# One PSUM tile for each row tile of a down product, in a state-space and SwiGLU kernel on one core

## The chip, the cores and the metric

The kernel runs on one core of a Trainium2 chip. The metric is the device time of one launch in microseconds. A kernel is timed in several runs; the profile is of one further execution, which has a time of its own.

## The reference, cut to what matters

Four layers follow each other on a row of 2048 positions with 512 channels: a state-space convolution (A), a SwiGLU feed-forward product (B), and both again with the same weights.

```python
x = A_u                                        # 1 x 2048 x 512
for _ in range(2):
    x = x + A(layernorm(x))                    # y = irfft(rfft(x) * rfft(K)), K from A, B, C, dt; + x * Dskip
    n = layernorm(x)
    x = x + (silu(n @ w_gate) * (n @ w_up)) @ w_down     # 512 -> 1376 -> 512
```

## The kernel before, in words

**Stages.** About the first 320 us make the convolution kernel, transform it, and split the weights into pairs of 16-bit halves. Behind it lie eight pairs of a convolution and a feed-forward product, in the order of the table `SEQ`: a layer and a block of 512 positions each. The loop at the end of the listing calls `ssm` for the next pair (all of it, line by line of the program) and then `ffn` for the present one, so that VectorE works on the convolution of one block while TensorE works on the feed-forward product of the block before.

**The order.** Nothing from there on is in an order written by hand. A scheduler with a timeline of its own sorts the instructions of each engine at build time: by program order, with the instructions under `tc.high_priority` ahead, and with whatever is ready by its own reckoning put into a wait. On the chip each engine then runs its list strictly in that order. So a change of one dependence moves many instructions on every engine.

**The feed-forward product.** `ffn` takes a block in two subtiles of 256 positions (`s`), each of two row tiles of 128 positions (`r`). For one subtile:

- `ffn_norm` normalizes the rows, splits them into two halves `nh` and `nlo`, and has them transposed by DMA (L841, tile `mix<-nn`).
- Gate and up: six groups `f0` of columns, each into a PSUM tile `pgu` of two banks. The group `FT - 1` is the remainder of 96 columns (`remainder`, L853 to L855, 48 matmuls with 96 columns); the other five have 48 matmuls with 256 columns (L886 to L888). Behind each group stands a chain: ScalarE silu (L891), VectorE product (L892), ScalarE cast into `hh` (L893), VectorE difference into `hl` (L894); for the remainder L861 to L864 and four transposing DMAs (L867).
- Down: for each row tile 33 matmuls with 512 columns (L900, L901, L902: eleven blocks `f` by three products of halves) into PSUM. Then VectorE adds the result to the rows `xt` (L905, called the eviction here), and a DMA writes them out (L907 in the last layer, else L909).

**PSUM.** The eight banks are shared by two tags. `sml` has four tiles of one bank, used by the convolution's products `pf` (L270) and `pi` (L781). `big` has two places of two banks each. Every `pgu` takes one of the two places, and so does the tile `py` of a down product: `py` has a bank for each of the two row tiles. A place is free for the next tile when all readers of the last one are done. A matmul into a tile, and a read of it by another engine, are ordered by the framework.

In `ffn` of the listing the groups stand in the order remainder, 0, 2, 4, 6, 8, then the down product. The last groups' chain must end before the down product's blocks 8 and 9 can be multiplied.

Of the kernel before, what the change touches and what calls it, by code (L numbers as in the profile page):

```python
# [16 lines left out]
OP = mybir.AluOpType  # L17
# [4 lines left out]
L, D, F = 2048, 512, 1376  # L22
P = 128
T = 512
NB = L // T
FT = 11
# [55 lines left out]
def kernel(ctx, tc, x, a_re, a_im, b_re, b_im, c_re, c_im, log_dt, d_skip,  # L82
                           w_gate, w_up, w_down, c_ef, c_ei, c_ek, c_am, c_eh, c_eih, out):
    nc = tc.nc
    V, A, G, PE = nc.vector, nc.scalar, nc.gpsimd, nc.tensor
# [9 lines left out]
    def tl(shape, name, tag, dt=F32):  # L95
        return sb.tile(shape, dt, name=name, tag=tag, bufs=BUFS[tag])

    def pbig(shape, name):
        return ps.tile(shape, F32, name=name, tag="big", bufs=2)
# [33 lines left out]
    sc6 = sb.tile([P, 6], F32, name="sc6")  # L133
# [158 lines left out]
    def second(h, q, space=psml):  # L292
        n = []
        for cp in range(2):
            t = tl([P, 2, HD], "n1", "w")
            nc.sync.dma_start(t, ndr[h, cp])
            n += [t[:, 0], t[:, 1]]
        return direct(1, h, q, n, space)
# [327 lines left out]
    def wgu(wi, kc, lo, n=1):  # L626
        u = 8 * wi + 4 * lo + kc
        v = wsl[u // 6].rearrange("p (u f) -> p u f", u=6)
        return v[:, u % 6] if n == 1 else v[:, u % 6:u % 6 + n]

    def wd(fc, lo):
        r = 2 * fc + lo
        if r < 5:
            return wsl[2][:, 4 * F + r * D:4 * F + (r + 1) * D]
        return wsl[3][:, (r - 5) * D:(r - 4) * D] if r < 21 else wx
# [177 lines left out]
    def ffn_norm(layer, b, s, wait=None):  # L813


        rows = TB // P
        xt = xs[SEQ.index((layer, b)) % 3][:, s * rows:(s + 1) * rows]
        nh, nlo = nhl2[:, s % 2, 0], nhl2[:, s % 2, 1]
        with tc.high_priority(offset=BOOST):
            if wait:  # L820
                rs, nb = stats(xt, rows, 256.0, "stats2")
                pt = pbig([P, rows, 4, P], "pt")
                for r in range(rows):
                    nn = nn2[:, r]
                    A.activation(nn, xt[:, r], AF.Identity, scale=rs[:, r:r + 1], bias=nb[:, r:r + 1])
                    for k in range(4):
                        PE.transpose(pt[:, r, k], nn[:, k * P:(k + 1) * P], ident)
                ptv = pt.rearrange("p r k t -> p k r t")
                nhv = nh.rearrange("p k (r t) -> p k r t", r=rows)
                A.activation(nhv, ptv, AF.Copy)  # L830
                wait()
                V.tensor_tensor(nlo.rearrange("p k (r t) -> p k r t", r=rows), ptv, nhv, OP.subtract)  # L832
                return nh, nlo
            rs, nb = row_stats(xt, rows, 256.0, "stats2", lambda r: nn2[:, r])
            nt = nn2[:, 1].bitcast(F16).rearrange("p (i k) -> p i k", i=2)
            for r in range(rows):
                A.activation(nn2[:, 0], xt[:, r], AF.Identity, scale=rs[:, r:r + 1], bias=nb[:, r:r + 1])
                A.activation(nt[:, 0], nn2[:, 0], AF.Copy)
                V.tensor_tensor(nt[:, 1], nn2[:, 0], nt[:, 0], OP.subtract)
                for i, o in enumerate((nh, nlo)):  # L840
                    nc.sync.dma_start_transpose(o[:, :, r * P:(r + 1) * P], nt[:, i])  # L841
        return nh, nlo

    def remainder(pgu, nh, nlo, hh, hl):

        rows = TB // P
        fs = slice(F - FR, F)
        pr = pgu.rearrange("p a b t -> p (a b t)")[:, :rows * 2 * FR].rearrange("p (r w f) -> p r w f", r=rows, w=2)
        for r in range(rows):
            rc = slice(r * P, (r + 1) * P)  # L850
            for wi in range(2):
                for k in range(4):
                    PE.matmul(pr[:, r, wi], lhsT=nh[:, k, rc], rhs=wgu(wi, k, 0)[:, fs], start=k == 0, stop=False)  # L853
                    PE.matmul(pr[:, r, wi], lhsT=nh[:, k, rc], rhs=wgu(wi, k, 1)[:, fs], start=False, stop=False)
                    PE.matmul(pr[:, r, wi], lhsT=nlo[:, k, rc], rhs=wgu(wi, k, 0)[:, fs], start=False, stop=k == 3)  # L855
        with tc.high_priority(offset=BOOST):
            both = tl([P, 2, TB], "sgr", "sg")
            sg = both[:, 0, :rows * FR].rearrange("p (r f) -> p r f", r=rows)
            hs = both[:, 1].bitcast(F16).rearrange("p (l r f) -> p l r f", l=2, r=rows)
            G.memset(hs[:, :, :, FR:], 0.0)  # L860
            A.activation(sg, pr[:, :, 0], AF.Silu, scale=sc6[:, 3:4])  # L861
            V.scalar_tensor_tensor(sg, pr[:, :, 1], sc6[:, 4:5], sg, OP.mult, OP.mult)
            A.activation(hs[:, 0, :, :FR], sg, AF.Copy)
            V.tensor_tensor(hs[:, 1, :, :FR], sg, hs[:, 0, :, :FR], OP.subtract)  # L864
            for i, o in enumerate((hh, hl)):
                for r in range(rows):
                    nc.sync.dma_start_transpose(o[:, FT - 1, r * P:(r + 1) * P], hs[:, i, r])  # L867

    def ffn(layer, b, ready=None):
        for s in range(T // TB):  # L870
            rows = TB // P
            xt = xs[SEQ.index((layer, b)) % 3][:, s * rows:(s + 1) * rows]
            nh, nlo = ready if ready and s == 0 else ffn_norm(layer, b, s)
            hh = tl([P, FT, TB], "hh", "hh", F16)
            hl = tl([P, FT, TB], "hl", "hl", F16)
            for f0 in (0, 2, 4, 6, FT - 1, 8) if ready and s == 0 else (FT - 1, 0, 2, 4, 6, 8):
                pgu = pbig([P, 2, 2, TB], "pgu")
                if f0 == FT - 1:
                    remainder(pgu, nh, nlo, hh, hl)
                    continue  # L880
                for i in range(2):
                    fs = slice((f0 + i) * P, (f0 + i + 1) * P)
                    for wi in range(2):
                        o = pgu[:, wi, i]
                        for k in range(4):
                            PE.matmul(o, lhsT=wgu(wi, k, 0)[:, fs], rhs=nh[:, k], start=k == 0, stop=False)  # L886
                            PE.matmul(o, lhsT=wgu(wi, k, 0)[:, fs], rhs=nlo[:, k], start=False, stop=False)  # L887
                            PE.matmul(o, lhsT=wgu(wi, k, 1)[:, fs], rhs=nh[:, k], start=False, stop=k == 3)  # L888
                with tc.high_priority(offset=BOOST):
                    sg = tl([P, 2, TB], "sg", "sg")  # L890
                    A.activation(sg, pgu[:, 0], AF.Silu, scale=sc6[:, 3:4])  # L891
                    V.scalar_tensor_tensor(sg, pgu[:, 1], sc6[:, 4:5], sg, OP.mult, OP.mult)  # L892
                    A.activation(hh[:, f0:f0 + 2], sg, AF.Copy)  # L893
                    V.tensor_tensor(hl[:, f0:f0 + 2], sg, hh[:, f0:f0 + 2], OP.subtract)  # L894
            py = pbig([P, rows, D], "py")
            for r in range(rows):
                rc = slice(r * P, (r + 1) * P)
                for f in range(FT):
                    n = min(P, F - f * P)
                    PE.matmul(py[:, r], lhsT=hh[:n, f, rc], rhs=wd(f, 0)[:n], start=f == 0, stop=False)  # L900
                    PE.matmul(py[:, r], lhsT=hh[:n, f, rc], rhs=wd(f, 1)[:n], start=False, stop=False)  # L901
                    PE.matmul(py[:, r], lhsT=hl[:n, f, rc], rhs=wd(f, 0)[:n], start=False, stop=f == FT - 1)  # L902
                c = s * rows + r
                with tc.high_priority(offset=BOOST):
                    V.scalar_tensor_tensor(xt[:, r], py[:, r], sc6[:, 5:6], xt[:, r], OP.mult, OP.add)  # L905
                    if layer == NL - 1:
                        nc.sync.dma_start(out[0, b * T + c * P:b * T + (c + 1) * P, :], xt[:, r])  # L907
                    else:
                        nc.sync.dma_start(xdr[b, c], xt[:, r])  # L909
# [15 lines left out]
    with tc.manual_schedule(engines={mybir.EngineType.Activation, mybir.EngineType.DVE, mybir.EngineType.PE}):  # L925
# [55 lines left out]
        for i in range(NCH - 1):  # L981
# [47 lines left out]
            if more:  # L1029
                f = second(*sec[i])  # L1030
# [110 lines left out]
    for i, lb in enumerate(SEQ):  # L1141
        if i + 1 < len(SEQ):
            take(ssm(*SEQ[i + 1]), 100)
        ffn(*lb, ready if i == 0 else None)
# [38 lines left out]
```

## Time and profile before

| | us |
|---|---|
| three runs | 2940.31, 1191.75, 1187.15; median 1191.75 |
| the profiled execution, its time | 1189.7 |
| its span, first to last instruction | 1187.9 |
| TensorE busy, share of the span | 1108.9, 93% |
| VectorE busy, share of the span | 1017.2, 86% |
| ScalarE busy, share of the span | 621.3, 52% |
| matmuls of the down products, L900, L901 and L902 together | 394.0 in 1024 of them that were recorded |
| evictions L905 | 32 of about 0.74 each |

In a profile a matmul's duration runs to the modelled end of its way through the array, so that matmuls that follow each other overlap; how far apart they start is read from the timeline. "Idle before" is the time in which the engine ran nothing ahead of an instruction, and the name behind it is what ended that time. PE is TensorE, DVE VectorE, ACT ScalarE, POOL GpSimd, SP the engine whose queue issues most DMAs; PEclk is the clock that TensorE was granted, as a share of its full one.

### The profile page before, as it was taken

The page shows a single profiled execution, that of the slowest core. Times are in us where ns is not written, and L with a number is a line of the kernel's source. Part 1 is how long each engine was busy: PE and PEld are TensorE (multiplying, and loading weights), DVE is VectorE, ACT ScalarE, POOL GpSimd, SP SyncE. Part 2 cuts the span into 40 slices and gives each one's busy share as a digit, 9 for nine tenths or more (in the row PEclk, how much of TensorE's full clock was granted, in tenths as well). Part 3 has the DMA queues.
Part 4 walks back from the last instruction along what each step waited for, and adds up shares of the span by engine and source line. Part 5 has one row for each costly group of instructions (what it writes and reads, how often), then busy time and mean ns, then how long its engine had stood idle before and what let it go on. Part 6 is the DMA issues. An engine that isn't in the chain of part 4 may idle for free.

```text
span 1187.9 us, 25243 instructions
## 1 busy us (share of the span) xinstructions
PE 1108.9 (93%) x10268; PEld 862.1 (73%) x10268; DVE 1017.2 (86%) x1669; ACT 621.3 (52%) x1190; POOL 112.9 (10%) x166
## 2 busy tenths in 40 slices
PE   2999899889789989899999999999999999999998
PEld 2867677677675848687768687858687686877875
DVE  8979999998899998999999999989992899983211
ACT  6999889862383553538553534735432452334211
POOL 3100200004200010001000100111000010000000
PEclk9989999999899989999999999989999999999999
DMA  6445455577695238332343444324534144312000
GB/s 235 124 139 127 119 124 124 128 191 197 193 282 170 76 115 200 114 103 83 103 151 122 121 167 144 105 77 155 153 105 135 45 121 134 120 41 46 14 23 18
DMA packets 138455, 146.90 MB, mean 124 GB/s; under 512 B 77858, under 2 KB 87074, under 8 KB 138339
## 3 DMA queue, kind: packets, MB, share of 16 engines
q1 hardware_dynamic: 133474, 128.51, 36.0%
q0 software_dynamic: 4864, 16.78, 6.1%
q8 instruction: 80, 1.31, 0.5%
q14 instruction: 37, 0.30, 0.1%
HBM read 98.19 MB, written 28.31 MB: 106 GB/s over the span
## 4 chain that ended last, share of the span: by engine, by line
PE 37%; DVE 24%; issue 4%; ACT 3%; DMA 3%; SPq 1%; POOL 1%; DVEq 0%; ACTq 0%; POOLq 0%
PE pgu L886 5%; PE pgu L887 5%; PE pgu L888 5%; PE py L900 5%; PE py L901 5%; PE py L902 4%; DVE t L762 4%; PE pi L781 3%; DVE yk L765 3%; PE pf L270 3%; DVE z L226 2%; DVE yk L762 2%; DMA mix<-nn 2%; DVE sg L892 2%; DVE hl L894 2%
## 5 line engine op out<-in xcount | busy, mean ns | idle before, releaser
L886 PE MATMUL pgu<-mix,wsl 128*128 128x256 f16 x1280 | 351.1, 274 | 4.6 <-DVE mix L832 2.4
L887 PE MATMUL pgu<-mix,wsl 128*128 128x256 f16 x1280 | 351.1, 274 | 0.0
L888 PE MATMUL pgu<-mix,wsl 128*128 128x256 f16 x1280 | 350.9, 274 | 0.0
L900 PE MATMUL py<-wsl,hh 128*128 128x512 f16 (+1 forms) x352 | 135.4, 385 | 9.3 <-DVE xg L905 4.7
L887 PEld LDWEIGHTS <-wsl 128*128 128x128 f16 x1280 | 125.9, 98 | 22.2 <-issue 5.9
L886 PEld LDWEIGHTS <-wsl 128*128 128x128 f16 x1280 | 126.0, 98 | 16.6 <-issue 0.3
L902 PE MATMUL py<-wsl,hl 128*128 128x512 f16 (+1 forms) x352 | 135.3, 384 | 2.7 <-DVE hl L894 2.7
L888 PEld LDWEIGHTS <-wsl 128*128 128x128 f16 x1280 | 126.0, 98 | 15.4
L901 PE MATMUL py<-wsl,hh 128*128 128x512 f16 x320 | 123.3, 385 | 0.0
L762 DVE TENSOR_TENSOR t<-uu,w 128x1024 f32<-128x1024 f32 x96 | 116.7, 1216 | 0.2
L765 DVE TENSOR_TENSOR yk<-yk,t 128x1024 f32<-128x1024 f32 x96 | 116.6, 1215 | 0.1
L891 ACT ACTIVATE sg<-pgu,sc 128x512 f32<-128x512 f32 x80 | 54.4, 680 | 106.5 <-PE pgu L888 100.2
L892 DVE SCALAR_TENSOR_TENSOR sg<-pgu,sc,sg 128x512 f32<-128x512 f32 x80 | 59.5, 744 | 50.6 <-ACT sg L891 50.4
L781 PE MATMUL pi<-yl,mix 128*128 128x256 f16 x672 | 91.6, 273 | 8.6 <-ACT yl L770 6.8
L547 PE MATMUL pw<-kt,ek 128*128 128x256 f32 (+2 forms) x420 | 95.9, 365 | 0.0
L893 ACT ACTIVATE hh<-sg 128x512 f16<-128x512 f32 x80 | 50.0, 626 | 78.5 <-DVE sg L892 78.3
L547 PEld LDWEIGHTS pw<-kt,ek 128*128 128x128 f32 x420 | 76.3, 190 | 9.1
L270 PE MATMUL pf<-z,eh 128*128 128x256 f16 x576 | 76.0, 273 | 0.0
L770 ACT ACTIVATE yl<-mix,sy 128x512 f16<-128x512 f32 x56 | 40.2, 718 | 64.5 <-DVE mix L767 64.3
L781 PEld LDWEIGHTS <-mix 128*128 128x128 f16 x672 | 65.1, 98 | 12.1 <-issue 2.2
L762 DVE TENSOR_TENSOR yk<-u,w0r 128x1024 f32<-128x1024 f32 x56 | 68.0, 1215 | 0.9 <-ACT u L272 0.9
L901 PEld LDWEIGHTS <-hh 128*128 128x128 f16 (+1 forms) x352 | 34.8, 99 | 46.4 <-issue 11.8
(247 smaller groups left out, 2182.9 us busy)
## 6 DMA issues: line engine op xcount, KB each, us to landing
w<-wdr SPq DMA_DIRECT2D x96, 256.0 KB, 2.7
uu<-udr SPq DMA_DIRECT2D x96, 256.0 KB, 3.0
udr<-u POOLq DMA_DIRECT2D x32, 256.0 KB, 2.5
wdr<-wo SPq DMA_DIRECT2D x96, 64.0 KB, 2.7
udr<-u SPq DMA_DIRECT2D x16, 256.0 KB, 2.2
g<-tmp POOLq DMA_DIRECT2D x8, 512.0 KB, 4.5
g<-btl POOLq DMA_DIRECT2D x8, 512.0 KB, 5.9
n<-xdr SPq DMA_DIRECT2D x4, 1024.0 KB, 5.6
```

The source lines that it names most:

```text
L270: PE.matmul(pf[:, o], lhsT=e, rhs=m, start=k == 0, stop=k == len(terms) - 1)
L547: PE.matmul(pw[:, i], lhsT=e, rhs=kt[:, :, c + 4 * k0:4 * k1:4, :].rearrange("p g k d -> p k g d"), start=c == 0, stop=c == 3)
L762: V.tensor_tensor(t, uu.unsqueeze(1).to_broadcast([P, 2, 2, HD]), w.unsqueeze(2).to_broadcast([P, 2, 2, HD]), OP.mult)
L765: V.tensor_tensor(yk, yk, t, OP.add)
L781: PE.matmul(pi[:, o], lhsT=e, rhs=m, start=k == 0, stop=k == len(terms) - 1)
L886: PE.matmul(o, lhsT=wgu(wi, k, 0)[:, fs], rhs=nh[:, k], start=k == 0, stop=False)
L887: PE.matmul(o, lhsT=wgu(wi, k, 0)[:, fs], rhs=nlo[:, k], start=False, stop=False)
L888: PE.matmul(o, lhsT=wgu(wi, k, 1)[:, fs], rhs=nh[:, k], start=False, stop=k == 3)
L892: V.scalar_tensor_tensor(sg, pgu[:, 1], sc6[:, 4:5], sg, OP.mult, OP.mult)
L900: PE.matmul(py[:, r], lhsT=hh[:n, f, rc], rhs=wd(f, 0)[:n], start=f == 0, stop=False)
L901: PE.matmul(py[:, r], lhsT=hh[:n, f, rc], rhs=wd(f, 1)[:n], start=False, stop=False)
L902: PE.matmul(py[:, r], lhsT=hl[:n, f, rc], rhs=wd(f, 0)[:n], start=False, stop=f == FT - 1)
```

## The change

Each row tile of a down product allocates a `py` of its own from the tag `big`, with one bank, inside the loop over `r`. The arithmetic and the number of instructions are the same.

```diff
-            py = pbig([P, rows, D], "py")
             for r in range(rows):
+                py = pbig([P, D], "py")
                 rc = slice(r * P, (r + 1) * P)
                 for f in range(FT):
                     n = min(P, F - f * P)
-                    PE.matmul(py[:, r], lhsT=hh[:n, f, rc], rhs=wd(f, 0)[:n], start=f == 0, stop=False)
+                    PE.matmul(py, lhsT=hh[:n, f, rc], rhs=wd(f, 0)[:n], start=f == 0, stop=False)
...
-                    V.scalar_tensor_tensor(xt[:, r], py[:, r], sc6[:, 5:6], xt[:, r], OP.mult, OP.add)
+                    V.scalar_tensor_tensor(xt[:, r], py, sc6[:, 5:6], xt[:, r], OP.mult, OP.add)
```

A tile of one bank still takes a whole place of the tag, which is as large as its largest tile. So a down product now holds both places of `big`, and before it held one.

The scheduler's lists are the same up to the first down product. From there on they differ. Three places show how, all on TensorE. A name has the number of its tile behind it; `wsl` and `wx` hold the weights, and the row with `wx` is the last block but one matmul of a row tile.

The end of the first row tile in the second down product, before. `py_4612` is the one tile of both row tiles, `pgu_5224` the remainder of the next subtile:

```order
L901 MATMUL py_4612<-wx_97,hh_4281 128x512
L902 LDWEIGHTS hl_4282
L902 MATMUL py_4612<-wsl3_3119,hl_4282 128x512
L853 LDWEIGHTS mix_2910
L853 MATMUL pgu_5224<-wsl0_3116,mix_2910 128x96
L854 LDWEIGHTS mix_2910
L854 MATMUL pgu_5224<-wsl0_3116,mix_2910 128x96
L900 LDWEIGHTS hh_4281
L900 MATMUL py_4612<-wsl2_3118,hh_4281 128x512
L901 LDWEIGHTS hh_4281
```

The same place in the change. `py_4613` is the tile of the first row tile, `py_4649` that of the second:

```order
L901 MATMUL py_4613<-wx_97,hh_4282 128x512
L902 LDWEIGHTS hl_4283
L902 MATMUL py_4613<-wsl3_3119,hl_4283 128x512
L902 LDWEIGHTS hl_4283
L902 MATMUL py_4649<-wsl3_3119,hl_4283 128x512
L900 LDWEIGHTS hh_4282
L900 MATMUL py_4649<-wsl3_3119,hh_4282 128x512
```

Before, the second row tile begins behind the first one's end, with two matmuls of the next remainder ahead of it. In the change 26 of its 33 matmuls stand ahead of the first one's end, and the remaining seven right behind it.

The last down product, at the end of the first row tile, before:

```order
L901 MATMUL py_13499<-wx_97,hh_13168 128x512
L902 LDWEIGHTS hl_13169
L902 MATMUL py_13499<-wsl3_3119,hl_13169 128x512
L900 LDWEIGHTS hh_13168
L900 MATMUL py_13499<-wsl2_3118,hh_13168 128x512
```

And in the change:

```order
L901 MATMUL py_13514<-wx_97,hh_13183 128x512
L902 LDWEIGHTS hl_13184
L902 MATMUL py_13514<-wsl3_3119,hl_13184 128x512
L901 LDWEIGHTS hh_13183
L901 MATMUL py_13550<-wsl3_3119,hh_13183 128x512
L902 LDWEIGHTS hl_13184
L902 MATMUL py_13550<-wsl2_3118,hl_13184 128x512
```

Here nothing else is left to run. In the change the second row tile is in its third block when the first one ends.

The end of the third down product, before, where the first full group of the next subtile (`pgu_5704`) follows the second row tile:

```order
L901 MATMUL py_5553<-wx_97,hh_5222 128x512
L902 LDWEIGHTS hl_5223
L902 MATMUL py_5553<-wsl3_3119,hl_5223 128x512
L886 LDWEIGHTS wsl0_3116
L886 MATMUL pgu_5704<-mix_2910,wsl0_3116 128x256
```

And in the change, where it is the remainder (`pgu_5648`):

```order
L901 MATMUL py_5591<-wx_97,hh_5224 128x512
L902 LDWEIGHTS hl_5225
L902 MATMUL py_5591<-wsl3_3119,hl_5225 128x512
L853 LDWEIGHTS mix_2910
L853 MATMUL pgu_5648<-wsl0_3116,mix_2910 128x96
```

The remainder of the next subtile, 48 matmuls, began between the two row tiles in all 15 down products that have a next subtile, and now begins behind both in all 15. The next full group follows the remainder. Between the end of the first row tile and the remainder stand 7 to 30 matmuls of the second row tile, and in most some of the convolution's. Between the end of the second row tile and the full group stand the 48 of the remainder alone in five of the 15; those 48 with 11 to 24 of the convolution's in nine; and 26 of the remainder with 13 of the convolution's in one, the second.

More of the change, by code (lines that the diff above doesn't have):

```diff
@@ L899, in ffn @@
                     n = min(P, F - f * P)
-                    PE.matmul(py[:, r], lhsT=hh[:n, f, rc], rhs=wd(f, 0)[:n], start=f == 0, stop=False)
-                    PE.matmul(py[:, r], lhsT=hh[:n, f, rc], rhs=wd(f, 1)[:n], start=False, stop=False)
-                    PE.matmul(py[:, r], lhsT=hl[:n, f, rc], rhs=wd(f, 0)[:n], start=False, stop=f == FT - 1)
+                    PE.matmul(py, lhsT=hh[:n, f, rc], rhs=wd(f, 0)[:n], start=f == 0, stop=False)
+                    PE.matmul(py, lhsT=hh[:n, f, rc], rhs=wd(f, 1)[:n], start=False, stop=False)
+                    PE.matmul(py, lhsT=hl[:n, f, rc], rhs=wd(f, 0)[:n], start=False, stop=f == FT - 1)
                 c = s * rows + r
                 with tc.high_priority(offset=BOOST):
-                    V.scalar_tensor_tensor(xt[:, r], py[:, r], sc6[:, 5:6], xt[:, r], OP.mult, OP.add)
+                    V.scalar_tensor_tensor(xt[:, r], py, sc6[:, 5:6], xt[:, r], OP.mult, OP.add)
                     if layer == NL - 1:
```

## The prediction

> **What bounds the kernel now.** I read the page's busy line first, then busy time by stage, then who waited for whom on TensorE, then the timeline at each wait that touches a down product.
>
> ```profile
> span 1187.9 us, 25243 instructions
> PE 1108.9 (93%) x10268; PEld 862.1 (73%) x10268; DVE 1017.2 (86%) x1669; ACT 621.3 (52%) x1190; POOL 112.9 (10%) x166
> ```
>
> Busy time by stage, with TensorE's first and VectorE's third:
>
> ```profile
> 0.00:320.00 320.00, 274.99 (x3348) 221.45 (x3348) 292.48 (x482) 238.17 (x464) 55.37 (x93) 0.98 0.56 150
> 320.00:1188.00 868.00, 833.93 (x6920) 640.65 (x6920) 724.75 (x1187) 383.16 (x727) 57.50 (x73) 0.98 0.38 114
> ```
>
> ```profile
> 530.00:640.00 110.00, 108.70 (x927) 85.12 (x925) 107.58 (x198) 65.78 (x133) 9.21 (x13) 1.00 0.37 114
> 1080.00:1140.00 60.00, 60.00 (x491) 42.49 (x489) 15.36 (x24) 13.35 (x23) 1.11 (x3) 1.00 0.09 25
> ```
>
> Up to 320 us no down product has run, and the change touches nothing there. Behind it TensorE works 834 of 868 us: 34 us are idle. VectorE is nearly full in the middle, but it runs ahead: from 1080 us it has 15 us of work in 60, while TensorE has no idle time left. So the end is set by TensorE's work behind 320 us and by what it loses there, and an idle stretch that goes away brings the end nearer by its length, as long as TensorE has inputs to go on with.
>
> TensorE's waits, by who ended them (total, times, longest):
>
> ```profile
> PE py L900 <- DVE xg L905: 4.7, 4, 2.5
> PE py L900 <- DVE xf L905: 3.7, 3, 1.6
> PE py L902 <- DVE hl L894: 2.7, 2, 2.0
> PE pgu L853 <- DMA mix<-nn: 2.0, 1, 2.0
> PE pgu L886 <- DVE xg L905: 0.7, 1, 0.7
> ```
>
> Seven times in 16 down products a matmul L900 stood until an eviction L905 was done: 8.4 us. The wait is plain in the last down product:
>
> ```profile
> 1175.29 0.38 PE L902 MATMUL py<-wsl,hl 96*128 96x512 f16 x1
> 1175.70 0.75 DVE L905 SCALAR_TENSOR_TENSOR xg<-py,sc,xg 128x512 f32<-128x512 f32 x1 [4.20 <-PE py L902]
> 1176.51 0.38 PE L900 MATMUL py<-wsl,hh 128*128 128x512 f16 x1 [0.84 <-DVE xg L905]
> ```
>
> The second row tile writes the other bank of `py`, and yet its first matmul starts 0.06 us after the first row tile's eviction has ended (1175.70 + 0.75 = 1176.45). So the tile is guarded as a whole: row tile 1 may not start until row tile 0 is read. In the other nine cases enough other work stood between.
>
> **Part 1: the wait that is removed.** With a tile each, row tile 1 needs only a free place, which the gate and up group before the last one left long ago or the last one leaves during row tile 0. What is one such wait worth? How far apart matmuls start comes from this stretch:
>
> ```profile
> 1090.60 0.38 PE L902 MATMUL py<-wsl,hl 96*128 96x512 f16 x1
> 1090.82 0.21 PE L854 MATMUL pgu<-wsl,mix 128*128 128x96 f16 x1
> 1092.52 0.21 PE L855 MATMUL pgu<-wsl,mix 128*128 128x96 f16 x1
> 1092.56 0.38 PE L900 MATMUL py<-wsl,hh 128*128 128x512 f16 x1
> 1099.47 0.38 PE L902 MATMUL py<-wsl,hl 96*128 96x512 f16 x1
> 1099.68 0.27 PE L886 MATMUL pgu<-mix,wsl 128*128 128x256 f16 x1
> ```
>
> 33 matmuls of 512 columns take 1092.56 to 1099.47, 32 steps of 0.216 us; the 41 of the remainder take 1090.82 to 1092.52, 40 steps of 0.0425. A matmul is shown with 0.38 us, so an idle stretch behind one of 512 columns is longer than the row says by 0.38 - 0.216 = 0.16 us. Seven waits: 8.4 + 7 x 0.16 = 9.5 us. In the changed order at least seven matmuls of row tile 1 stand behind row tile 0's end, and they wait for no eviction; so I take all of it: **-9.5 us**. The bounds are 0 (each wait comes back at the next place) and -9.5.
>
> **Part 2: the second down product.** One of the seven waits stands beside another:
>
> ```profile
> 432.64 0.38 PE L902 MATMUL py<-wsl,hl 96*128 96x512 f16 x1
> 435.02 0.22 PE L853 MATMUL pgu<-wsl,mix 128*128 128x96 f16 x1 [2.01 <-DMA mix<-nn]
> 435.50 0.74 DVE L905 SCALAR_TENSOR_TENSOR xg<-py,sc,xg 128x512 f32<-128x512 f32 x1
> 436.29 0.58 PE L900 MATMUL py<-wsl,hh 128*128 128x512 f16 x1 [1.01 <-DVE xg L905]
> ```
>
> Two matmuls of the next remainder were put between the row tiles, and their transposed input landed late: 2.0 us idle. Behind it the clock was halved, as the windows that I laid around the slow matmuls here and at a second place show (the column behind TensorE's time):
>
> ```profile
> 435.48:442.31 6.83, 6.02 (x15) 0.50 0.64 175
> 783.64:790.46 6.82, 6.19 (x28) 0.50 0.34 115
> ```
>
> At half clock 6.83 us do the work of 3.4. In the changed order 26 matmuls of row tile 1 come before row tile 0's end and the remainder behind both, so nothing waits at 432 us: -2.0 and -3.4. But the remainder's second half needs the last transposes:
>
> ```profile
> 437.10 3.19 SPq L841 DMA_TRANSPOSE mix<-nn  x2
> ```
>
> ```profile
> mix<-nn SPq DMA_TRANSPOSE x60, 2.5
> ```
>
> The last one is issued about 437.10 + 3.19 - 1.2 = 439.1 and lands 2.5 us later, at 441.6 (estimated from these two rows). With part 3's steps: row tile 0's end moves back by 26 x 0.216 = 5.6 us, from 432.6 to 438.2; then come 7 x 0.216 of row tile 1, 13 x 0.109 of the convolution and 24 x 0.0425 of the remainder's first half, 3.9 us, which makes 442.1. That is just behind the landing, so I charge nothing: **-5.4 us**; the bounds are that and 0.
>
> [...]
>
> **Part 3: the new wait.** Before, the next remainder took the second place of `big` while the down product ran, and a full group followed row tile 1 at once (1099.47, then 1099.68 above). Now both places are taken. The remainder needs row tile 0 evicted, and the full group behind it needs row tile 1 evicted or the remainder read. An eviction with nothing ahead of it costs 1176.51 - 1175.29 - 0.22 = 1.0 us from when TensorE could have gone on. The worst one of the trace:
>
> ```profile
> 497.01 0.38 PE L902 MATMUL py<-wsl,hl 96*128 96x512 f16 x1
> 497.36 1.36 PE L781 MATMUL pi<-yl,mix 128*128 128x256 f16 x11
> 498.56 0.21 PE L854 MATMUL pgu<-wsl,mix 128*128 128x96 f16 x1
> 498.71 1.42 DVE L226 SCALAR_TENSOR_TENSOR bt<-n 128x256 f32<-128x256 f32 x4
> 500.05 1.21 DVE L762 TENSOR_TENSOR t<-uu,w 128x1024 f32<-128x1024 f32 x1
> 501.19 0.74 DVE L905 SCALAR_TENSOR_TENSOR xg<-py,sc,xg 128x512 f32<-128x512 f32 x1
> 501.98 0.38 PE L900 MATMUL py<-wsl,hh 128*128 128x512 f16 x1 [2.54 <-DVE xg L905]
> ```
>
> VectorE's own list held four L226 and an L762 ahead of the eviction: 501.98 - 497.01 - 0.22 = 4.75 us. What stands in front of the wait now: for the full group the 48 of the remainder, 48 x 0.0425 = 2.04 us, and in nine of 15 places 11 to 24 of the convolution's matmuls at (498.56 - 497.36) / 11 = 0.109, so 3.2 to 4.7; for the remainder at least the seven matmuls of row tile 1 with 13 of the convolution's, 2.9. In the quiet end 2.04 covers 1.0: nothing. In the busy middle a worst-case eviction shows 4.75 - 2.04 = 2.7 us where only the remainder stands before it. I charge one such case in the run: **+2.7 us**. Low bound 0; high bound: three of the five places with only the remainder lie in the busy part, and the second place is near them, so 4 x 2.7 = 10.9.
>
> While TensorE waits there, only matmuls of this list are held, and VectorE has the convolution to go on with; nothing new is queued on its side.
>
> [...]
>
> **What stays.** The work: 33 matmuls and one eviction of 0.74 us for each row tile as before. The other idle stretches behind 320 us, some 868.0 - 833.9 - 8.4 - 2.0 = 24 us, hang on chains in front of the down products or in the convolution, such as this one:
>
> ```profile
> 782.58 0.39 PE L902 MATMUL py<-wsl,hl 128*128 128x512 f16 x1 [2.04 <-DVE hl L894]
> ```
>
> Here block 8's `hl` was late, and the second slow window followed. In the new order matmuls of row tile 1 stand in that place instead of the remainder's, for about as long. I count no gain and no loss, and keep 2.0 + 3.4 = 5.4 us for the range.
>
> **The sum,** against the profiled execution's 1189.7 (span 1187.9 and 1.8 around it): 1189.7 - 9.5 - 5.4 + 2.7 = **1177.5 us**. The median of the three runs is 1191.75, 2 us above it, and the fastest 1187.15; I keep the profile's base.
>
> **The rivals.**
>
> *The inputs are the bound in the early part.* Parts of the gain lie before the first layer's third block, whose transposed inputs came just in time:
>
> ```profile
> 546.77 8.68 SPq L841 DMA_TRANSPOSE mix<-nn  x4
> ```
>
> ```profile
> 556.42 0.21 PE L853 MATMUL pgu<-wsl,mix 128*128 128x96 f16 x1
> ```
>
> The last transpose is issued at 555.4 and the remainder that reads them starts at 556.42. If TensorE comes earlier and the inputs don't, the 1.0 + 2.5 + 2 x 0.16 = 3.8 us of the two early waits and the 5.4 of part 2 are given back: 1177.5 + 9.2 = 1186.7. Against it: in the new order the remainder starts behind row tile 1, a down product's half later (7.1 us), which leaves room for just about that gain. Chance 0.26.
>
> *More goes than I count.* Row tile 1 as cover also fills the wait for block 8's `hl`, and no new wait comes: 1177.5 - 2.7 - 5.4 = 1169.4. For it: a matmul of row tile 1 is five times as long as one of the remainder. Against it: the scheduler puts cover in by its own clock, and VectorE was late against that clock. Chance 0.14.
>
> *The lost place.* The full group, or the remainder, stands for evictions in the busy middle, and the waits are long enough to halve the clock. The place: TensorE's L886 behind row tile 1. The price: four times 2.7 + 3.4 = 24.4 us in place of my 2.7, so 1177.5 - 2.7 + 24.4 = 1199.2, slower than before. It decides from new waits and slow windows above 9.5 + 5.4 = 14.9 us. For it: 4.75 us for one eviction, on a VectorE that is 98% busy from 530 to 640 us (107.58 of 110). Against it: nine of the 16 first evictions made nobody wait. Chance 0.12.
>
> *The change doesn't do what it says.* If row tile 1 already ran beside the eviction, nothing would move: 1189.7. The rows at 1176.45 and 1176.51 speak against it. Chance 0.03.
>
> **How the numbers follow.** My forecast has 0.45, the rivals the rest. The time is that of the forecast, 1177.5. The range takes the -5.4 of the untouched stretches and the bound of part 3 at zero on one side, with a few us for an order that is new on every engine: 1166. On the other it takes in the inputs' case, and most of the way to the lost place: 1197. A difference of 2%, 24 us, is about what a measurement of this kernel can tell from no change. Faster by that means 1166 or less and takes nearly all the untouched stretches: 0.05. Slower by that means 1213 or more, beyond the lost place's price: 0.04. Within: 0.91.
>
> **What would show it.** In the profile after, L900's waits for L905 are gone from TensorE's list, and row tile 1's matmuls stand before row tile 0's eviction. No slow window lies behind the second down product, at about 435 us. L886 and L853 have waits for L905 of some 3 us together; 15 or more would mean the lost place. Idle time of TensorE behind 320 us falls from 34 to about 26 us. The prediction is wrong if L900 still waits for L905, if the new waits exceed the old ones, or if the time moves while these waits don't, which would put the cause in the new order of the other engines.

## The result, and the profile after

The changed kernel takes **1178.1 us** (median of six runs, 1176.46 to 1180.78); the kernel before takes 1189.37 beside it (six runs). The ratio is 0.9909 with a 95% interval of 0.9882 to 0.9936: about 1% faster, and 1 lies outside the interval. That is finer than the 2% which the prediction took for the limit of what a measurement can tell here. The prediction was 1177.5. The profiled execution took 1176.5 us, with this span:

```profile
span 1174.7 us, 25246 instructions
PE 1101.3 (94%) x10268; PEld 859.9 (73%) x10268; DVE 1018.3 (87%) x1669; ACT 622.1 (53%) x1190; POOL 117.0 (10%) x166
```

The span is 13.2 us shorter. The window view from 366 us, where the first down product begins, says which part of that is idle time. Its columns are the stretch and its length, the busy time of TensorE, of its weight loads, VectorE, ScalarE and GpSimd, then TensorE's clock, the DMA share and GB/s. Before:

```profile
366.00:1190.00 824.00, 796.29 (x6600) 608.45 (x6599) 682.45 (x1130) 350.80 (x678) 53.15 (x67) 0.99 0.35 104
```

After:

```profile
366.00:1190.00 824.00, 788.10 (x6600) 605.81 (x6599) 684.25 (x1130) 352.35 (x680) 55.34 (x67) 1.00 0.34 104
```

The same 6600 matmuls need 8.2 us less busy time. To the end of the span the idle time is 1187.9 - 366 - 796.29 = 25.6 us before and 1174.7 - 366 - 788.10 = 20.6 us after. So the 13.2 us are **5.0 of idle time and 8.2 of busy time, nearly all of it half clock**. Behind 366 us, three stretches of the profile before in which TensorE worked ran at half clock (0.50), from 367.21, 435.48 and 783.64 us, with TensorE busy for 3.42, 6.02 and 6.19 us. Half of that sum, 7.8 us, is an estimate of what the full clock would have saved: 796.29 - 7.8 = 788.5, close to the 788.10 after, where no stretch behind 366 us ran at half clock (1.00 from there to the end of the span). The first of the three, 1.7 us, is not the change's doing: it follows waits between 363.8 and 366.5 us, and up to the first down product the lists are the same.

TensorE's waits behind 366 us after, all that the view lists (total, times, longest):

```profile
PE pi L781 <- ACT yl L770: 4.2, 3, 1.7
PE pgu L855 <- DMA mix<-nn: 2.6, 1, 2.6
PE pgu L886 <- DVE xg L905: 2.4, 2, 1.7
PE pgu L886 <- DVE sg L892: 1.9, 2, 1.7
PE pf L270 <- DVE z L226: 1.7, 2, 1.1
PE pgu L886 <- DVE xf L905: 1.5, 1, 1.5
PE pgu L853 <- DMA mix<-nn: 1.1, 1, 1.1
PE pi L781 <- DVE yl L226: 0.7, 1, 0.7
PE pf L270 <- ACT z L260: 0.5, 1, 0.5
```

No row of L900 is left. Before, seven waits of L900 for L905 made 8.4 us. In their place L886 waits for L905, 3.9 us in three places, where it was 0.7 in one. At the last down product, first TensorE's timeline:

```profile
1164.57 0.38 PE L902 MATMUL py<-wsl,hl 96*128 96x512 f16 x1
1164.78 0.38 PE L901 MATMUL py<-wsl,hh 128*128 128x512 f16 x1
```

Then VectorE's:

```profile
1164.98 0.75 DVE L905 SCALAR_TENSOR_TENSOR xg<-py,sc,xg 128x512 f32<-128x512 f32 x1 [5.72 <-PE py L902]
```

The last matmul of row tile 0 is followed 0.21 us later by one of row tile 1, while the eviction of row tile 0 has not even begun. The guard on the whole tile is gone.

### The profile page after: what moved, and what is told of

The parts are those of the page before. It is cut to its first block, busy times and chain, and to the rows that moved or that the text cites. A ratio compares the mean times of both kernels' runs of the same rounds, so it can differ in the third digit from the quotient of the medians.

```text
span 1174.7 us, 25246 instructions
## 1 busy us (share of the span) xinstructions
PE 1101.3 (94%) x10268; PEld 859.9 (73%) x10268; DVE 1018.3 (87%) x1669; ACT 622.1 (53%) x1190; POOL 117.0 (10%) x166
## 4 chain that ended last, share of the span: by engine, by line
DVE 40%; PE 33%; issue 10%; ACT 9%; DMA 5%; POOL 2%; SPq 1%; DVEq 0%; ACTq 0%; POOLq 0%
DVE t L762 5%; PE pgu L886 5%; PE pgu L887 5%; PE pgu L888 5%; DVE yk L765 4%; PE pw L547 4%; DVE yk L762 3%; DVE z L226 3%; PE pi L781 3%; PE py L900 2%; PE py L901 2%; PE py L902 2%; DVE sg L892 2%; DVE bt L226 2%; DVE yl L226 2%
## 5 line engine op out<-in xcount | busy, mean ns | idle before, releaser
L886 PE MATMUL pgu<-mix,wsl 128*128 128x256 f16 x1280 | 349.7, 273 | 9.0 <-DVE sg L892 2.6
L888 PEld LDWEIGHTS <-wsl 128*128 128x128 f16 x1280 | 125.5, 98 | 14.8
L886 PEld LDWEIGHTS <-wsl 128*128 128x128 f16 x1280 | 125.6, 98 | 14.7
L900 PE MATMUL py<-wsl,hh 128*128 128x512 f16 (+1 forms) x352 | 133.0, 379 | 0.0
L902 PE MATMUL py<-wsl,hl 128*128 128x512 f16 (+1 forms) x352 | 132.2, 379 | 0.0
L901 PE MATMUL py<-wsl,hh 128*128 128x512 f16 x320 | 120.8, 379 | 0.0
L781 PE MATMUL pi<-yl,mix 128*128 128x256 f16 x672 | 93.7, 274 | 5.9 <-ACT yl L770 5.1
L270 PE MATMUL pf<-z,eh 128*128 128x256 f16 x576 | 75.1, 273 | 2.2 <-DVE z L226 1.7
L781 PEld LDWEIGHTS <-mix 128*128 128x128 f16 x672 | 65.9, 99 | 14.7 <-issue 1.1
L894 DVE TENSOR_TENSOR hl<-sg,hh 128x512 f16<-128x512 f32 x80 | 55.2, 692 | 13.5 <-ACT hh L893 13.5
```

The costliest lines, as they stand in the source:

```text
L781: PE.matmul(pi[:, o], lhsT=e, rhs=m, start=k == 0, stop=k == len(terms) - 1)
L900: PE.matmul(py, lhsT=hh[:n, f, rc], rhs=wd(f, 0)[:n], start=f == 0, stop=False)
L901: PE.matmul(py, lhsT=hh[:n, f, rc], rhs=wd(f, 1)[:n], start=False, stop=False)
L902: PE.matmul(py, lhsT=hl[:n, f, rc], rhs=wd(f, 0)[:n], start=False, stop=f == FT - 1)
```

## The experiments

**The theory**: the two-bank tile was guarded as a whole, and the change gains what its waits cost, on TensorE and through TensorE's clock, less what the lost place of `big` costs. **The rivals**: the gain comes from the scheduler's new order and not from the guard; the lost place is what still holds the kernel back, so a version that gives row tiles a place elsewhere gains more. Ratios are to the kernel before, run beside the experiment (1187.2 to 1187.5 us).

Each run lists its span and mean granted clock c. The table calls (1 - c) times the span the clock's part, and the rest of the run's time the rest. In the profile before the slow stretches ran at 0.50, so there the clock's part is half their length. Means over the runs of each kernel, in us:

| kernel | rest | clock's part |
|---|---|---|
| before (24 runs) | 1168.1 | 19.6 |
| the change (6) | 1163.2 | 15.1 |
| e2, first four pairs | 1164.9 | 14.8 |
| e3, last four pairs | 1165.8 | 17.6 |
| e4, before with rows swapped | 1169.3 | 17.6 |
| e5, before with a late eviction | 1174.2 | 18.9 |
| e6, change with a late eviction | 1163.6 | 12.6 |
| e8, change with rows swapped | 1163.1 | 14.9 |
| e9, change with group first | 1161.0 | 18.5 |
| e10, before with group first | 1166.0 | 16.6 |
| e12, three one-bank places | 1172.1 | 24.4 |
| e11, remainder in one bank | 1180.6 | 35.2 |
| e7, second row tile in one bank | 1189.2 | 33.6 |
| e1, both row tiles in one bank | 1192.4 | 42.6 |

Between before and the change the means differ by 9.4 us, 4.9 in the rest and 4.5 in the clock's part. The second isn't a price in full. In the profile before 13.7 of its 22.9 us lie ahead of 366 us, in the profile of the change all of its 15.4, and the change touches nothing there. A straight line through the 24 runs of before gives 0.47 us of time for 1 us of the clock's part. So these sums don't settle how much of the gain is clock. The pair of profiles above, with 8.2 us of it, shows a large draw.

### The guard: a late eviction (e5, e6)

The direct test: make the first eviction of the last pair late and see who stands. Four reads of `py` that nobody uses go ahead of it; e5 does this to the kernel before, e6 to the change (with `py` for `py[:, r]`).

```diff
                 with tc.high_priority(offset=BOOST):
+                    if (layer, b) == SEQ[-1] and r == 0:
+                        for _ in range(4):
+                            V.tensor_scalar(tl([P, D], "late", "t1", BF16), py[:, r], 1.0, None, OP.mult)
+                with tc.high_priority(offset=BOOST):
                     V.scalar_tensor_tensor(xt[:, r], py[:, r], sc6[:, 5:6], xt[:, r], OP.mult, OP.add)
```

> The kernel before; in the last pair (the last two down products) four more VectorE readers of row tile 0's result, whose own result nobody uses, stand ahead of its eviction. VectorE is idle there, so they only make the eviction later, by some 4 x 0.7 = 2.8 us (estimated from the eviction's own 0.75). Theory (one common tile guards row tile 1 against row tile 0's eviction): L900 waits some 3.6 us in the last down product instead of 0.84, and some 2 us in the one before, where 1.7 us of remainder matmuls stand between; 5 us longer than before, more if the clock is halved behind the waits. Rival (row tile 1 waits for something else that ends at the same time): before's time within 1 us.

> The same four readers in the changed kernel. Theory: row tile 1 runs on, and the remainder, which needs row tile 0's place, comes 5.6 us behind row tile 0's end, so nothing waits; the change's time, 1178, within 1 us, and no wait of TensorE in the last two down products. Rival (the wait has only been moved to the next tile that needs the place): 2 to 5 us longer than the change, with waits in L853.

e5 measured 1193.07 us, ratio 1.004 [1.0021, 1.006], 5.7 us above before by the medians, where the theory had 5; e6 1176.05, ratio 0.9894 [0.9861, 0.9927], within noise of the change. In e5 the eviction is L909, and these are all of TensorE's waits in the last two down products (1100 us to the end):

```profile
PE py L900 <- DVE xg L909: 4.7, 2, 3.2
```

Before, the same stretch has one wait of 0.8 us. In e6 it has none at all, though VectorE's timeline shows the same delay:

```profile
1163.28 2.48 DVE L907 TENSOR_SCALAR late<-py 128x512 bf16<-128x512 f32 x4 [5.71 <-PE py L902]
1165.68 0.74 DVE L909 SCALAR_TENSOR_TENSOR xg<-py,sc,xg 128x512 f32<-128x512 f32 x1
```

2.5 us of delay raised the common tile's wait in the last down product from 0.84 to 3.2 us and brought one of 1.5 us in the down product before; the separate tiles waited for nothing. The time grew by 5.7 us where the waits of this pair grew by 3.9; no row here places the other 1.8 us. This shows the guard, in one pair, apart from any new order.

### Half of the program (e2, e3)

e2 gives own tiles to the first four pairs, e3 (`>= 4`) to the last four; the others keep one common tile.

```diff
+            split_py = SEQ.index((layer, b)) < 4
+            both = None if split_py else pbig([P, rows, D], "py")
             for r in range(rows):
-                py = pbig([P, D], "py")
+                py = pbig([P, D], "py") if split_py else both[:, r]
```

> Own tiles only in the first four pairs of the table (down products 1 to 8), one common tile in the last four. Theory: the waits of L900 for L905 that lie at 436, 502, 617 and 672 us before (6.4 us by the rows, 7.1 with the overlap) go, the slow windows near 435 and 784 us (6.8 us of time) too; new waits near 501 and 784 us of 2.3 us come; so 9 to 11 us faster than before, ratio 0.991 to 0.993, nearly all of the change's gain. Rival (the gain is spread over all 16 down products, or is an accident of the whole order): about half of the gain, 5 to 6 us, or a value not tied to it.

> Own tiles only in the last four pairs (down products 9 to 16). Theory: only the waits at 843, 997 and 1177 us go (2.0 us, 2.5 with the overlap), and a new one of 1.5 us near 995 us comes; so 0 to 2 us faster than before, ratio 0.998 to 1.000, and the slow windows near 435 and 784 us stay. Rival (spread evenly): 5 to 6 us faster, ratio 0.995.

e2: 1179.6, ratio 0.9939 [0.9918, 0.9961]. e3: 1182.11, ratio 0.9965 [0.9943, 0.9987]. The lines stand two lower in these kernels, so the down product's first matmul is L902 and the eviction L907. Waits of e2:

```profile
PE py L902 <- DVE xg L907: 3.1, 3, 1.8
PE py L902 <- DVE xf L907: 0.8, 1, 0.8
```

Waits of e3:

```profile
PE py L902 <- DVE xf L907: 3.0, 2, 1.7
PE py L902 <- DVE xg L907: 2.9, 2, 1.8
```

In e2 all of these lie behind 700 us, in e3 all before 750: the waits stay where the tile is common and go where it isn't. The first half brings 7.9 us by the medians, between the theory's 9 to 11 and the rival's 5 to 6; the interval, 4.6 to 9.7 us, reaches into both. The second half brings 5.4 us by the medians and 4.4 by the means. That is near the rival's 5 to 6 and not the theory's 0 to 2, though its interval, 1.5 to 6.8 us, excludes neither. The waits don't account for it: those of L900 fell from 8.4 to 5.9 us, and that of L886 for L907 rose from 0.7 to 2.1. Nor are the slow windows those of before alone: e3's profile has one from 998.90 us (clock 0.50), where the profile before has none. Whether the two near 435 and 784 us stayed, as the theory had it, no row here shows. So the waits show where the guard is, but not how the gain is spread over the program; that stays open.

### The order alone (e4, e8)

e4 is the kernel before, e8 the change, with the row tiles in the other order. This gives the scheduler a new order, with the guard as it was.

```diff
-            for r in range(rows):
+            for r in reversed(range(rows)):
```

> A control for the order: the kernel before with the two row tiles of a down product taken in the other order; the common tile and its guard stay. Theory: the same waits, 7 to 10 us of L900 for L905, and the time of before within 3 us (ratio 0.997 to 1.003). Rival (any new order moves the time by chance as much as the change did): 5 us or more away from before in either direction.

> A control for the order on the changed side: the changed kernel with the row tiles taken in the other order. Theory: no wait of L900 for L905, and the change's ratio of 0.991 within 0.003. Rival (the change's gain is an accident of its order): a ratio of 0.997 or more.

e4: 1186.78, ratio 0.9994 [0.9974, 1.0014]; e8: 1177.1, ratio 0.9918 [0.9886, 0.9951]. e4 keeps its waits:

```profile
PE py L900 <- DVE xg L905: 4.7, 4, 2.5
PE py L900 <- DVE xf L905: 3.6, 3, 1.5
```

e8 has none of them. This new order by itself is worth nothing, and the change's gain doesn't hang on which row tile comes first. It is a mild test: e4's waits for the eviction, 8.3 us in seven, are nearly those of before. A larger change of order, e10 below, is worth 5 us with the guard in place.

### Where row tiles or the remainder take a one-bank place (e1, e7, e11, e12)

Three versions keep both places of `big` for the groups, by taking places from the tag `sml`. e1 puts both row tiles there:

```diff
-                py = pbig([P, D], "py")
+                py = psml([P, D], "py")
```

> Each row tile's py comes from the tag of four one-bank places (sml) instead of the tag of two two-bank places, so the guard between the row tiles stays removed and no place of a gate and up group is taken. Theory (guard removed, place lost): L900 waits for no eviction, and the 3.8 us that L886 waits for L905 in the change go too; idle time of TensorE behind 366 us falls to about 12 us; time 3 to 4 us below the change, about 1174 to 1175, ratio to before 0.986 to 0.988. Rival one (the convolution needs its four one-bank places): pi and pf wait for evictions instead, 3 us or more, and the time is at or above the change's 1178. Rival two (any new order moves the time by chance): anything from 1170 to 1195, without tie to these waits.

e1: 1235.54, ratio 1.0407 [1.0379, 1.0435]. The theory's 1174 was wrong. Rival one was right about the time and about who stands, `pi` and `pf`, but not about what they wait for. Waits of e1:

```profile
PE pi L781 <- ACT yl L770: 40.3, 10, 7.9
PE pf L270 <- ACT z L260: 7.2, 1, 7.2
```

No wait for an eviction is left, on either side, but the convolution's own matmuls now wait: its work in e1's middle stage has slid back, as VectorE's busy time there shows (the change, then e1, each from its windows).

```profile
530.00:860.00 330.00, 323.97 (x2746) 252.64 (x2745) 321.23 (x547) 172.11 (x339) 32.58 (x36) 1.00 0.41 125
```

```profile
530.00:860.00 330.00, 308.04 (x2511) 234.75 (x2509) 282.09 (x477) 155.14 (x296) 22.88 (x31) 0.96 0.36 108
```

e7 puts only the second row tile there, e11 only the remainder, with row tiles as in the change.

```diff
-                py = pbig([P, D], "py")
+                py = (psml if r else pbig)([P, D], "py")
```

```diff
-                pgu = pbig([P, 2, 2, TB], "pgu")
...
-                    remainder(pgu, nh, nlo, hh, hl)
+                    remainder(psml([P, 2 * (TB // P) * FR], "pgr"), nh, nlo, hh, hl)
...
+                pgu = pbig([P, 2, 2, TB], "pgu")
```

> Row tile 0's py from the two-bank tag as in the change, row tile 1's from the one-bank tag. Theory (the first experiment's loss came from down products holding one-bank places of the convolution): half as many such places are held, so a part of that loss comes back, 10 to 30 us above the change, with L781 waiting for yl again. Rival (one of the four places is to spare, only two are not): no two-bank place is lost, so 1 to 4 us below the change, about 1175.

> The changed kernel with the remainder's gate and up tile, 384 columns, in the one-bank tag, so that a two-bank place is free for the next full group once row tile 0 is evicted. Theory (lost place): the waits of L886 for L905, 3.9 us, go, and if a one-bank place for some 3 us does not hold up the convolution, the time is 3 to 4 us below the change, about 1174, ratio 0.987 to 0.989. Rival (the one-bank places are all needed): L781 and L270 wait for evictions or yl, and the time is above the change, 1180 or more.

e7: 1223.25, ratio 1.0307 [1.0264, 1.0351]; e11: 1215.17, ratio 1.0249 [1.0214, 1.0285]. e7 lost 45 us against the change, more than the 10 to 30 of its theory, and e11 lost 37, where its theory had a gain of 3 to 4; its rival, a loss with waits for `yl`, held. Waits of e7:

```profile
PE pi L781 <- ACT yl L770: 26.4, 6, 9.4
```

and of e11:

```profile
PE pi L781 <- ACT yl L770: 9.4, 7, 3.7
PE py L900 <- DMA hh<-sgr: 6.7, 5, 2.6
```

e12 asks for the price of one such place by itself: the change with `sml` cut to three.

```diff
-        return ps.tile(shape, F32, name=name, tag="sml", bufs=4)
+        return ps.tile(shape, F32, name=name, tag="sml", bufs=3)
```

> The changed kernel with three one-bank places instead of four; nothing else takes the bank. It prices one such place by itself. Theory (the convolution needs them): slower than the change by 5 us or more, with waits in L781 and L270. Rival (one is to spare): the change's 1178 within 2 us; then the loss of the first experiment has another cause, such as the scheduler's order.

e12: 1196.54, ratio 1.009 [1.0059, 1.0121]: 18 us above the change, for a place that is taken all the time. Not all of that bears on e1, e7 and e11. The first gate and up matmul starts at 336.1 us, in the change at 325.5, so 10.6 of the 21.6 us between the two spans arise ahead of any down product, where e1, e7 and e11 lose nothing (their first one starts at 324.8 to 325.0). And the waits that the theory named didn't grow; in L781 they are shorter than the change's, and others came:

```profile
PE pgu L853 <- DMA mix<-nn: 6.0, 2, 3.8
PE pi L781 <- ACT yl L770: 3.7, 2, 3.1
```

So in these two profiles a place less costs 11.0 us from the first gate and up matmul on, and how it comes to that isn't shown. It doesn't split the 45 us of e7, where a row tile holds a place only for a part of the time but other matmuls are ordered differently too. What else e1, e7 and e11 lose stays open.

### A group ahead of the remainder (e9, e10)

In the change the remainder, 2.0 us, is in five of 15 places all that stands between row tile 1 and the full group that needs its place. e9 lets a full group come first, so that the remainder waits instead; e10 does the same to the kernel before.

```diff
-            for f0 in (0, 2, 4, 6, FT - 1, 8) if ready and s == 0 else (FT - 1, 0, 2, 4, 6, 8):
+            for f0 in (0, 2, 4, 6, FT - 1, 8) if ready and s == 0 else (0, FT - 1, 2, 4, 6, 8):
```

> The changed kernel with the first full group of gate and up ahead of the remainder, groups in the order 0, remainder, 2, 4, 6, 8. Behind row tile 1 then stand 48 matmuls of 256 columns, 5.2 us, ahead of the first one that needs row tile 1's place, instead of the remainder's 2.0 us. Theory (the new waits of L886 for L905, 3.9 us in the change's profile, are the price of the lost place): they go, L853 gets none, and the time is 3 to 4 us below the change, about 1174, ratio to before 0.987 to 0.989. Rival (these waits hide others that end at the same time, or the new order brings its own): the change's ratio of 0.991 or more.

> The control for the last one: the kernel before with the same order of groups, 0, remainder, 2, 4, 6, 8. Theory: L900 still waits for L905, since the guard is there, though the full group gives the scheduler other cover; before's time within 3 us, ratio 0.997 to 1.003. Rival (the order of the groups alone does what the change does): 6 us or more below before.

e9: 1179.38, ratio 0.9921 [0.9892, 0.995]; e10: 1182.2, ratio 0.9954 [0.9935, 0.9972]. Waits of e9:

```profile
PE pgu L886 <- DVE sg L892: 7.2, 6, 2.6
PE pgu L886 <- DVE xf L905: 2.2, 1, 2.2
PE pgu L886 <- DVE xg L905: 0.3, 1, 0.3
```

The new waits fell from 3.9 to 2.5 us, and the waits for the chain behind a group rose from 1.9 to 7.2. The time is within noise of the change's, so the theory's 3 to 4 us didn't come, and the rival held: these waits hide others, or the order brings its own. e10 came out between the expectations: the order of the groups is worth 5 us on the kernel before, with 3.1 us of L900's waits still there. So an order can be worth about half of the change's gain with the guard in place. The two edits don't add up; that both remove in part the same idle time would explain it, and isn't shown. No version beat the change: e6 and e8 are the nearest, and agree with it.

## Why the prediction was right, step by step

| step | predicted, us | in the two profiles |
|---|---|---|
| part 1, L900's waits | -9.5 | 8.4 in 7 to none; -9.5 with the 0.16 each |
| part 2, the wait of 2.0 us for transposes | -2.0 | 2.0 to 3.7: +1.7 |
| part 2, the first slow window | -3.4 | -3.4 |
| part 3, the new wait | +2.7 | L886 for L905, 0.7 to 3.9: +3.2 |
| what stays | 0 | `hl` 2.7 to none; the second slow window -3.4, and one of 1.7 that the change doesn't touch; other waits either way |
| sum against the profile's time | -12.2 | -13.2 |

**Part 1** held in its mechanism: all seven waits went, e5 and e6 show the guard, and e4 and e8 that the order of the row tiles isn't it. Its 1.1 us of overlap (seven times 0.16) can't be seen by themselves in any run.

**Part 2** was wrong where it charged nothing for the second half of the remainder. Nothing waits at 432 us, but TensorE's timeline at the second down product of the change has this a little later:

```profile
442.68 0.22 PE L853 MATMUL pgu<-wsl,mix 128*128 128x96 f16 x1 [1.13 <-DMA mix<-nn]
446.86 0.22 PE L855 MATMUL pgu<-wsl,mix 128*128 128x96 f16 x1 [2.61 <-DMA mix<-nn]
```

The step that failed is the landing at 441.6. I took the transposes' time from the profile before, as if TensorE's order didn't touch it. SP's queue in the change:

```profile
439.67 1.20 SPq L841 DMA_TRANSPOSE mix<-nn  x1
440.95 1.00 SPq L909 DMA_DIRECT2D xdr<-xg  x2
442.00 0.45 SPq L760 DMA_DIRECT2D uu<-udr  x1
443.30 1.30 SPq L841 DMA_TRANSPOSE mix<-nn  x1
```

The last transpose is issued at 443.3, where I had 439.1, and its reader starts at 446.86. VectorE's list tells why it is late:

```profile
439.13 0.75 DVE L905 SCALAR_TENSOR_TENSOR xg<-py,sc,xg 128x512 f32<-128x512 f32 x1
439.79 0.42 DVE L226 SCALAR_TENSOR_TENSOR t<-dd,bb 128x256 f32<-128x256 f32 x1
440.12 0.75 DVE L905 SCALAR_TENSOR_TENSOR xg<-py,sc,xg 128x512 f32<-128x512 f32 x1
440.78 1.22 DVE L762 TENSOR_TENSOR yk<-u,w0r 128x1024 f32<-128x1024 f32 x1
441.91 0.75 DVE L226 SCALAR_TENSOR_TENSOR yl<-mix,sy,yl 128x512 f16<-128x512 f32 x1
442.57 0.69 DVE L839 TENSOR_TENSOR nn<-nn 128x512 f16<-128x512 f32 x1
```

The last difference L839 that these transposes need stands behind both evictions and three instructions of the convolution, and starts at 442.57 us; before, it started at 438.38. The wait that I thought covered has only moved: TensorE is ahead of this chain, and what it saves at the row tiles it stands for at the remainder. From 366 to 470 us it is idle for 6.7 us before and 6.5 after. That was my first rival's mechanism (the inputs bound early), in the second down product and at 3.7 us, and not beyond it. (In that rival's own place, 555.4 us is where the last transpose's row ends; by the reckoning of part 2 it is issued 1.2 us earlier, at 554.2. Its chance and price don't hang on that.)

**The slow window** went away all the same, but not for my reason. I had tied it to the wait. (The two waits ahead of it lay 0.26 us apart: the first ends at 435.02, the second begins at 435.28.) After, the waits at this place are longer, 3.7 us for 3.0, and no window is slow; in e2 and e8, with much the same two waits (2.7 and 1.2 us, 2.6 and 1.2), one is. The rows are in the last section; what decides, they don't show.

**Part 3** held in size and in the place, L886 behind row tile 1, though in three smaller waits and not in one of 2.7 us. TensorE's timeline has the two large ones:

```profile
784.58 0.27 PE L886 MATMUL pgu<-mix,wsl 128*128 128x256 f16 x1 [1.74 <-DVE xg L905]
994.62 0.27 PE L886 MATMUL pgu<-mix,wsl 128*128 128x256 f16 x1 [1.49 <-DVE xf L905]
```

The third, 0.6 us, lies at 501 us, where I had looked for the worst. L853 has no such wait. The lost-place rival was the right mechanism at a small price.

**What stays** did move: block 8's `hl` no longer makes TensorE wait, as the rival of "more goes" said. So the sum is right partly because two errors meet: part 2's +3.7 and small new waits (L270 for `z`, 2.2 us; L886 for `sg`, from 0.7 to 1.9) against `hl` and the other slow windows. (The steps leave some 2.6 us of small terms; the list of waits is no finer than that, since its rows fall by 6.8 us and the idle time by 5.0.) Idle time behind 320 us fell from 34.0 to 29.0, where I had said 26, and TensorE's busy time behind 366 us fell by 8.2 us in the profiles, nearly all of it half clock, where I had 3.4. That the time came within 0.6 us of the forecast is luck: the mechanism of part 1 was right, and the rest of the sum was right by errors that cancel, of the clock above all, which I could price but not place.

## What to carry to other kernels

Where a framework orders accesses by tile, a tile with parts that are written and read apart ties these parts together: the writer's next part waits for the reader's last (here 8.4 us in seven waits, and none with a tile each), and a tile for each part frees it, even if a bank stays unused. Ask then where the places come from: the same edit gained 1% with places from one tag, and versions with places from the convolution's tag lost 2 to 4%, for reasons that the runs show only in part. And a time of arrival that is read from the profile before holds only for engines whose own order and inputs the change leaves alone.

## What the runs showed of the hardware

In the profile before, the 3.41 us ahead of the slow stretch from 435.48 us, the first 3.41 us of that stretch, and the 3.42 us ahead of the one from 783.64 us (TensorE's clock is the third figure from the right):

```profile
432.07:435.48 3.41, 1.20 (x7) 0.37 (x6) 3.41 (x7) 1.07 (x2) 0.00 (x0) 1.00 0.22 53
435.48:438.89 3.41, 2.60 (x7) 0.92 (x7) 3.40 (x7) 1.59 (x3) 0.00 (x0) 0.50 1.02 292
780.22:783.64 3.42, 1.38 (x13) 0.68 (x10) 3.42 (x10) 0.84 (x2) 0.00 (x0) 1.00 0.00 0
```

Ahead of the two slow stretches TensorE was busy for 1.20 and 1.38 us, at clock 1.00. In the change the wait of 2.6 us lies in two rows:

```profile
441.84:445.25 3.41, 1.57 (x14) 1.18 (x14) 3.41 (x7) 1.54 (x4) 0.20 (x1) 1.00 0.97 301
445.25:448.66 3.41, 1.80 (x30) 1.73 (x31) 3.41 (x7) 1.71 (x5) 0.00 (x0) 1.00 0.66 163
```

TensorE was busy for 1.57 and 1.80 us here, and the row behind, 448.66 to 452.08 us, has clock 1.00 too. In e2, whose waits for the transposes are 2.7 and 1.2 us:

```profile
445.38:448.80 3.42, 0.76 (x12) 0.47 (x10) 3.42 (x7) 1.21 (x5) 0.00 (x0) 1.00 0.86 186
448.80:452.21 3.41, 3.41 (x31) 2.80 (x28) 3.04 (x5) 2.26 (x7) 0.72 (x1) 0.50 0.91 328
```

TensorE was busy for 0.76 us of the first row, and the second ran at 0.50. e8 shows the like: 0.81 us busy from 449.40 to 452.81 us and then 3.41 us at 0.51.

So waits of like length had different prices: behind 3.0 us of waits in the profile before the half clock cost about 3 us more (half of 6.02 us busy at 0.50, an estimate), behind 3.9 us in e2 1.7 (half of 3.41), and behind 3.7 us in the change nothing. No run here moves such a wait by itself, so why they differ isn't shown. The clock differs between runs of one program too: over 24 runs of the kernel before its mean went from 0.976 to 0.990, 17 us by the clock's part, while their times lay within 10 us.
